# Two instructions of ScalarE moved behind a copy, and four half matmuls reordered, in the first attention of a fused attention-and-feed-forward kernel

## The chip, the cores and the metric

The kernel runs on one core of one Trainium2 chip. A core has five engines that run side by side, each in its own program order: TensorE (PE in the profile; its weight loads are PEld), VectorE (DVE), ScalarE (ACT), GpSimd (POOL) and SyncE (SP, which here only issues DMAs). They wait for one another through semaphores. The metric is the device time of one execution in microseconds (us).

## The reference

The input x has 2048 rows of 448. It is layer-normalised, and the result xn goes into two branches whose sum is added to x:

```python
xn = _layernorm(x)                                  # (x - mean) / sqrt(var + 1e-5)
# branch A: 16 heads of 28, causal attention over the last 256 positions
q, k, v = split(xn @ wqkv)
p = softmax(where(mask, q @ k.T * 28 ** -0.5, -1e9))
a = (p @ v) @ wo
# branch B
b = (gelu(xn @ w_gate) * (xn @ w_up)) @ w_down      # hidden width 1792
out = x + a + b
```

All arrays are bf16.

## The kernel before

The 2048 rows are 16 tiles of 128, handled in four blocks of 512 rows. For each block there is an attention stage (`attention`, 11 or 12 steps) and a gated feed-forward stage (`gated`); the other matmuls (q, k and v projections, up-projections, the previous block's down-projection) are fed into the attention steps so that PE has work while ACT computes exponentials. The order of instructions on every engine is the order in which the Python program emits them; there is no scheduler. Each engine runs its own in that order and waits at the first one whose input or buffer is not ready.

The width of 448 is three full chunks of 128 and one of 64. A projection is therefore three dense matmuls (`mm3`, L228) and one half matmul over 64 rows (`mm_half`, L233). Two half matmuls on different halves of the array can run at the same time, so halves are collected and issued in pairs ("excursions"): a generator yields HOLD after its dense part, and the next attention step first runs what is held. PE's results go to PSUM banks: tags "m" (two), "d" and "o" (one each), handed out in turn as m, m, d by `bank` during block 0. A bank is free again when the copy that empties it has run, on ACT or on DVE.

Block 0's attention has twelve steps, three for each group g of four heads. The one that the change touches is the beginning:

- Step 0 computes scores of group 0 (L600), the Exp on ACT (L604), zeroes masked entries on POOL (`masked`, L518), and feeds the dense q and k projections of group 1.
- Step 1 begins with the second excursion: the halves of q and k of group 1, and those of v for tiles 2 and 3, whose dense parts wait in banks "o" and "d"; then the copies out of PSUM: v of tile 3 on DVE (L253), q on ACT (L280), k on DVE (L281). Group 2's q projection takes bank "d", which v of tile 3 has held. After its scores, Exp and the dense projections of group 2, step 1 runs `ahead2`: statistics of tiles 6 and 7 on DVE (`stat`, L195 and L196), their reciprocal standard deviation on ACT (`rstd`: a Ln, L200, and an Exp, L201), the normalisation of tile 5 on DVE (`norm`, L209, a wide piece of 448 columns and a narrow one of 64) and its DMA transpose (L215, issued by SP).
- Step 2 begins with the third excursion, the halves of q and k of group 2 and their copies; then scores, Exp, and `ahead3` (norm and transpose of tiles 6 and 7, the copy of v of tile 2, and the loads of the remaining weights). Group 3's k projection takes bank "d", which group 2's q has held until its copy.
- At the end of steps 3 and 4 DVE runs `fill_pads`: nine small copies into unused columns of the q and k weights (L318 with 16 elements and L320 with 48, from `wraw` to `wqp` and `wkp`), and then three into `w3p` and a memset (L330). In steps 3 to 5 PE also computes up-projections (`ue`) of hidden chunks f = 2, 3, 8 and 9, which DVE casts into `hT` (L409), and the first `pv` (probabilities times v, L560), which DVE copies to `oc` (L570). From step 5 on follow the projections of block 1, v of tiles 4 and 5 first; v of tile 5 takes bank "d", which f = 8 has held.

The lines that only code can say, the bank order and the extra work of block 0:

```python
ring = [("m", "m", "d"), 0]
aux = [ahead, ahead2, ahead3, lambda: fill_pads(False), lambda: fill_pads(True), ...]
feeds = [Feed((gen_qk(0, (1, 2, 3), [(t, pvs[t]) for t in (2, 3)]), ...),
              (gen_up(0, (2, 8)), ...), (gen_proj(1), ...), (gen_up(0, (4,)), ...))]
```

Of the kernel before, what the change touches and what calls it, by code (L numbers as in the profile page):

```python
# [75 lines left out]
def kernel(  # L76
# [172 lines left out]
    def v_half(t, pv):  # L249
        mm_half(pv, xnT[:, 3, t * P:(t + 1) * P], wv[:, 3, :], t % 2, False, True)  # L250

    def v_copy(t, pv, copy):
        copy(out=v_sb[:, t, :, 0:Dh], in_=pv.rearrange("p (h d) -> p h d", d=Dh))  # L253
# [19 lines left out]
    def qk_halves(qb, g, pq, pk):  # L273
        w3 = w3p[:, 4 * g:4 * g + 4, :].rearrange("p h d -> p (h d)")
        for hi, ps in enumerate((pq, pk)):
            mm_half(ps, w3, xnT[:, 3, qb * QB:(qb + 1) * QB], hi, False, True)
# [7 lines left out]
    def gen_qk(qb, gs, others=()):  # L284

        for g in gs:
            pq = bank("pq")[:, :]
            proj(pq, wqp, qb, g)
            if qb and g == 3:
                yield 650  # L290
                ts = slice(qb * QB, (qb + 1) * QB)
                nc.tensor.matmul(pq, lhsT=w3p[:, 12:16, :].rearrange("p h d -> p (h d)"), rhs=xnT[:, 3, ts], start=False, stop=True,
                                 skip_group_check=True)
                nc.scalar.copy(out=qT[:, 3, ts], in_=pq)
                done.add((qb, 3))
                yield -220
                return
            yield 650
            pk = bank("pk")[:, :]
            proj(pk, wkp, qb, g)  # L300
            yield 650, HOLD
            qk_halves(qb, g, pq, pk)
            for t, pv in others:
                v_half(t, pv)
            if others:
                v_copy(*others[1], nc.vector.tensor_copy)
            qk_copies(qb, g, pq, pk)
            others = ()
            yield -360
# [211 lines left out]
    def attention(qb, feeds, aux, plan):  # L521
        oN = blk.tile([P, 4, QB], bf16, name="oN")
        oNs[qb] = oN
        parts, copied, inverses, later, fresh, behind = {}, [], [], [], [], []

        def scale_o(g, oc, inv):
            nc.gpsimd.tensor_tensor(out=oN[:, g, :], in0=oc[:, :], in1=inv, op=ALU.mult)  # L527

        def sums():

            g, oc = copied.pop(0)
            l1 = work.tile([P, 16, 32], f32, name="l1", tag="wc", bufs=1)
            ls = l_all[:, 4 * qb + g, :]
            nc.vector.transpose(out=l1[:, :, :].rearrange("p a b -> p (a b)"), in_=oc[:, :])  # L534
            nc.vector.tensor_copy(out=ls, in_=l1[:, :, Dh])
            ri = work.tile([P, 16], f32, name="ri")
            nc.vector.reciprocal(out=ri[:, :], in_=ls)
            inverses.append((g, oc, ri, l1))

        def inverse():  # L540

            g, oc, ri, l1 = inverses.pop(0)
            rb = l1 if qb else work.tile([P, 16, 32], f32, name="rb", tag="wb", bufs=1)
            nc.vector.transpose(out=rb[:, :, :], in_=ri[:, :].unsqueeze(2).to_broadcast([P, 16, 32]))  # L544
            later.append((g, oc, rb[:, :, :].rearrange("p a b -> p (a b)")))

        def add_halves(oc, ov):
            nc.scalar.copy(out=oc[:, :], in_=ov[0][:, :])  # L548
            nc.vector.tensor_tensor(out=oc[:, :], in0=oc[:, :], in1=ov[1][:, :], op=ALU.add)  # L549

        def pv(g):

            tags = ("o",) if not qb else ("m", "m" if g < 3 else down_tag[0])
            ov = [psum.tile([P, QB], f32, name="ov", tag=tag, bufs=2 if tag == "m" else 1) for tag in tags]
            todo = parts.pop(g)
            for n, (half, kt, q0, nq, col, p_sb) in enumerate(todo):
                k0 = 64 * half if half else 0
                r = slice(k0, k0 + (P if half is None else 64))
                for j in range(4):
                    nc.tensor.matmul(ov[half or 0][32 * j:32 * j + 32, q0:q0 + nq], lhsT=v_sb[r, kt, 4 * g + j, :],  # L560
                                     rhs=p_sb[r, j, col:col + nq], start=n == (half or 0), stop=n + len(tags) >= len(todo),
                                     tile_position=(k0, 32 * j), skip_group_check=True)
            oc = work.tile([P, QB], f32, name="oc", tag="wb" if qb and g % 2 else "wa", bufs=1)
            if qb:
                if g == 2:
                    behind.append((oc, ov))
                else:
                    add_halves(oc, ov)
            else:
                nc.vector.tensor_copy(out=oc[:, :], in_=ov[0][:, :])  # L570
            copied.append((g, oc))

        if qb:
            feeds[0].run()
        steps = list(steps_of(qb))
        pvs = {4: 0, 6: 1, 9: 2} if qb else {4: 0, 7: 1, 10: 2}
        for i, (scores, ncol, edges) in enumerate(steps):
            while (qb, scores[-1][0]) not in done:
                feeds[0].run()
            for fd in feeds:  # L580
                if fd.held:
                    fd.run()
            if i in pvs:
                pv(pvs[i])
            while fresh:
                apply_masks(*fresh.pop(0))
            if not qb and i - 1 in pvs:
                sums()
                inverse()
            if qb and i - 1 in pvs:  # L590
                sums()
            if qb and i - 2 in pvs:
                inverse()
            ss = phase[0].pool.tile([P, 4, QB], f32, name="sc", tag="s")
            p_sb = work.tile([P, 4, QB], bf16, name="p_sb", bufs=5)
            for g, half, kt, q0, nq, col in scores:
                k0, nk = (64 * half, 64) if half is not None else (0, P)
                for j in range(4):
                    r = slice(32 * j, 32 * j + Dh)
                    nc.tensor.matmul(ss[k0:k0 + nk, j, col:col + nq], lhsT=kT[r, g, kt * P + k0:kt * P + k0 + nk],  # L600
                                     rhs=qT[r, g, qb * QB + q0:qb * QB + q0 + nq], start=True, stop=True,
                                     tile_position=(32 * j, k0), skip_group_check=True)
                parts.setdefault(g, []).append((half, kt, q0, nq, col, p_sb))
            nc.scalar.activation(out=p_sb[:, :, 0:ncol], in_=ss[:, :, 0:ncol], func=ACT.Exp, scale=SCALE)  # L604
            while behind:
                add_halves(*behind.pop(0))
            if qb:
                fresh.append((p_sb, edges))
            else:
                for m in edges:  # L610
                    masked(p_sb, *m)
            while later:
                scale_o(*later.pop(0))
            left = len(steps) - i
            if left == 1:
                drain(feeds)
            elif not qb:
                share(feeds + [Feed()], 1e12, 0)
            else:
                to = plan.get(i, 0)  # L620
                whole = sum(f.left for f in feeds) + STEP * left + PV * sum(j > i for j in pvs)
                ahead = STEP + PV * (i + 1 in pvs) + (360 if to > 1000 else 0)
                late = 400 if i == 0 else 0
                want = (whole - late) / (left + 0.2) + late - ahead - to
                if i in pvs:
                    had = feeds[0].left
                    share(feeds[:1], min(1100, want), 0)
                    want -= had - feeds[0].left
                share(feeds, want, to)
            if aux:  # L630
                aux.pop(0)()

        def rest():
            while fresh:
                apply_masks(*fresh.pop(0))
            pv(3)

        def after(f):
            if inverses:
                inverse()  # L640
                scale_o(*later.pop(0))
            elif copied:
                sums()

        return rest, after
# [44 lines left out]
    pq, pk = (phase[0].pool.tile([P, 2, QB], f32, name="s0", tag="s")[:, 0, :] for _ in range(2))  # L690
# [23 lines left out]
    def ahead2():  # L714
        stat(6)
        stat(7)
        rstd(6, 2)
        norm(5)
        dma_transp(5)

# [211 lines left out]
```

## Time and profile before

| | |
|---|---|
| median of 3 runs | 223.24 us (223.16 to 223.36) |
| the profiled execution | 223.5 us |
| its span on the core | 221.7 us |
| PE busy | 214.3 us (97%) |
| DVE busy | 156.2 us (70%) |
| ACT busy | 132.9 us (60%) |
| POOL busy | 45.0 us (20%) |
| granted TensorE clock | 1.0 |

The span is the time from the first to the last instruction that the hardware profiler saw; the profiled execution's own time is 1.8 us longer. A line of a timeline has the start in us from the span's start, the duration in us, the engine, the source line, the operation, the tile written and those read, the shapes (partitions x elements), and how many instructions were merged; in brackets stands the idle time of the engine just before, and what ended it. In the chain of work that ended last, a line has start, length, engine, tile and source line. In the list of waits it has the waiting engine and instruction, what it waited for, us in total, how often, and the longest. The ends of matmuls are modelled.

### The profile page before, as it was taken

Reading aid. Unit: us, or ns where it says so; the run is one execution under the profiler, and the core shown is the slowest. Engines: PE = TensorE matmul, PEld = TensorE weight load, DVE = VectorE, ACT = ScalarE, POOL = GpSimd, SP = SyncE. Lnnn points to the kernel's source line nnn. Section 1 sums busy time; section 2 is a strip of 40 time slices with the busy share of each in tenths; the row PEclk is TensorE's granted clock in tenths of the full one; section 3 lists DMA queues with packets and bytes.
Section 4 is the critical chain, followed back from the end, with each engine's and each line's share of the span. In section 5 each row is a group of like instructions: output and inputs, shape, how many; then the busy total and the mean of one; then the engine's idle time right before and its main releaser. Section 6 shows DMA issues by size and latency. Waiting matters only on the chain.

```text
span 221.7 us, 5352 instructions
## 1 busy us (share of the span) xinstructions
PE 214.3 (97%) x2240; PEld 94.9 (43%) x2240; DVE 156.2 (70%) x370; ACT 132.9 (60%) x129; POOL 45.0 (20%) x65
## 2 busy tenths in 40 slices
PE   6999999999999999999999999999999999999992
PEld 2433333344444444444444445444344435444571
DVE  5889996799666983679566896495444899479320
ACT  4497788644878875432878886233567778464000
POOL 5773687320000220022000031022000022022000
PEclk9999999999999999999999999999999999999999
DMA  6997699104200001102500000200000000000011
GB/s 193 304 296 94 174 326 305 22 1 74 44 3 21 24 24 29 18 3 44 70 1 23 24 1 26 57 5 0 0 4 21 24 3 24 21 0 4 22 43 25
DMA packets 18044, 13.28 MB, mean 60 GB/s; under 512 B 8704, under 2 KB 16992, under 8 KB 18016
## 3 DMA queue, kind: packets, MB, share of 16 engines
q1 hardware_dynamic: 17072, 12.62, 22.6%
q8 instruction: 18, 0.29, 0.6%
q10 hardware_dynamic: 944, 0.29, 0.5%
q14 instruction: 10, 0.08, 0.1%
HBM read 9.15 MB, written 2.18 MB: 51 GB/s over the span
## 4 chain that ended last, share of the span: by engine, by line
PE 95%; DVE 2%; ACT 1%; POOL 0%; issue 0%; DVEq 0%
PE po L375 20%; PE gt L228 17%; PE u L228 12%; PE sc L600 6%; PE po L370 6%; PE gt L233 5%; PE ue L228 5%; PE ov L560 5%; PE pq L228 4%; PE pv L228 4%; PE pk L228 3%; PE wps L190 2%; PE pq L233 2%; PE ue L233 1%; PE pv L233 1%; PE s L228 1%
## 5 line engine op out<-in xcount | busy, mean ns | idle before, releaser
L604 ACT ACTIVATE p_sb<-sc 128x2048 bf16<-128x2048 f32 (+2 forms) x42 | 73.8, 1758 | 12.6 <-PE sc L600 7.3
L375 PE MATMUL po<-wd,hT 128*128 128x448 bf16 (+1 forms) x238 | 50.0, 342 | 0.0
L452 ACT ACTIVATE ge<-gt 128x1024 bf16<-128x1024 f32 x28 | 28.7, 1025 | 33.6 <-PE u L233 20.9
L527 POOL TENSOR_TENSOR oN<-oc,l 128x512 bf16<-128x512 f32 x12 | 16.0, 1332 | 138.6 <-DVE l L544 88.2
L228 PE MATMUL gt<-xnT,wg 128*128 128x512 bf16 x168 | 40.3, 380 | 0.0
L456 DVE TENSOR_TENSOR hT<-ge,u 128x512 bf16<-128x512 bf16 x40 | 25.6, 682 | 9.7 <-ACT ge L452 9.6
L375 PEld LDWEIGHTS <-hT 128*128 128x128 bf16 x238 | 21.4, 98 | 18.6 <-issue 2.6
L228 PE MATMUL u<-xnT,wu 128*128 128x512 bf16 x120 | 29.2, 379 | 0.0
L508 DVE TENSOR_TENSOR p_sb<-p_sb,masks 128x256 bf16<-128x256 bf16 (+1 forms) x90 | 27.2, 357 | 0.4 <-ACT p_sb L604 0.4
L228 PEld LDWEIGHTS <-wg 128*128 128x128 bf16 x168 | 15.1, 98 | 21.4 <-issue 5.2
L228 PEld LDWEIGHTS <-wu 128*128 128x128 bf16 x168 | 16.0, 98 | 19.2 <-issue 1.0
L549 DVE TENSOR_TENSOR oc<-oc,ov 128x512 f32<-128x512 f32 x12 | 8.3, 688 | 18.3 <-ACT oc L548 18.3
L600 PE MATMUL sc<-qT,kT 28*64 28x320 bf16 (+7 forms) x640 | 16.9, 263 | 0.1
L380 DVE TENSOR_TENSOR res<-po,x_sb 128x448 bf16<-128x448 f32 (+1 forms) x17 | 10.0, 586 | 8.7 <-PE po L375 8.6
L370 PE MATMUL po<-wo,oN 128*128 128x448 bf16 (+1 forms) x68 | 15.9, 342 | 0.0
L518 POOL TENSOR_SCALAR_AFFINE_SELECT p_sb<-p_sb 128x512 bf16<-128x512 bf16 (+1 forms) x20 | 14.3, 736 | 7.8 <-ACT p_sb L604 7.6
L409 DVE CAST hT<-ue 128x512 bf16<-128x512 f32 x16 | 10.2, 680 | 6.3 <-PE ue L233 6.2
L548 ACT COPY oc<-ov 128x512 f32<-128x512 f32 x12 | 7.0, 584 | 11.9 <-PE ov L560 11.9
L233 PE MATMUL gt<-xnT,wgu 64*128 64x512 bf16 x48 | 13.2, 379 | 0.0
L228 PE MATMUL pq<-xnT,wqp 128*128 128x512 bf16 x45 | 12.2, 380 | 0.3 <-DVE v_sb L253 0.3
L534 DVE STREAM_TRANSPOSE l<-oc 128x512 f32<-128x512 f32 x16 | 11.3, 704 | 1.4 <-POOL oN L527 1.2
L228 PE MATMUL ue<-xnT,wu 128*128 128x512 bf16 x48 | 12.0, 380 | 0.0
(87 smaller groups left out, 236.0 us busy)
## 6 DMA issues: line engine op xcount, KB each, us to landing
out_dram<-res SPq DMA_DIRECT2D x15, 112.0 KB
x_sb<-in_A_x_dram SPq DMA_DIRECT2D x3, 448.0 KB
wu<-in_B_w_up_dram SPq DMA_DIRECT2D x1, 1344.0 KB
wg<-in_B_w_gate_dram SPq DMA_DIRECT2D x1, 1344.0 KB
wd<-in_B_w_down_dram SPq DMA_DIRECT2D x3, 448.0 KB
wraw<-in_A_wqkv_dram SPq DMA_DIRECT2D x2, 252.0 KB
wo<-in_A_wo_dram SPq DMA_DIRECT2D x4, 98.0 KB
wv<-in_A_wqkv_dram SPq DMA_DIRECT2D x1, 336.0 KB
```

Source lines behind the costliest of these rows:

```text
L228: nc.tensor.matmul(ps, lhsT=lhs(c), rhs=rhs(c), start=start and c == 0, stop=stop and c == 2, skip_group_check=True)
L233: nc.tensor.matmul(ps, lhsT=lhs[p0:p0 + 64], rhs=rhs[p0:p0 + 64], start=start, stop=stop, tile_position=(p0, 0), skip_group_check=True)
L370: nc.tensor.matmul(po[:, 0:w], lhsT=oN[:, g, cs], rhs=wo[:, g, lo:up], start=(g == 0), stop=False, skip_group_check=True)
L375: nc.tensor.matmul(po[:, 0:w], lhsT=hT[:, f, cs], rhs=wd[:, f, lo:up], start=False, stop=(f == NF - 1), skip_group_check=True)
L452: nc.scalar.activation(out=ge[:, :, :], in_=pr["gt"][:, :, :], func=ACT.Gelu_apprx_tanh)
L456: nc.vector.tensor_tensor(out=hT[:, f + i, :], in0=ge[:, i, :], in1=u[:, :], op=ALU.mult)
L508: nc.vector.tensor_tensor(out=reg, in0=reg, in1=m, op=ALU.mult)
L518: nc.gpsimd.affine_select(out=reg, in_=reg, pattern=mid + [[1 if diag else -1, min(w, P)]], compare_op=ALU.is_ge, fill=0.0, base=0 if diag ...
L527: nc.gpsimd.tensor_tensor(out=oN[:, g, :], in0=oc[:, :], in1=inv, op=ALU.mult)
L534: nc.vector.transpose(out=l1[:, :, :].rearrange("p a b -> p (a b)"), in_=oc[:, :])
L600: nc.tensor.matmul(ss[k0:k0 + nk, j, col:col + nq], lhsT=kT[r, g, kt * P + k0:kt * P + k0 + nk], rhs=qT[r, g, qb * QB + q0:qb * QB + q0 + ...
L604: nc.scalar.activation(out=p_sb[:, :, 0:ncol], in_=ss[:, :, 0:ncol], func=ACT.Exp, scale=SCALE)
```

## The change

Two things in block 0's attention. In `gen_qk`, the halves of v for tiles 2 and 3 are issued ahead of the halves of q and k of group 1 (the order of the copies stays: v of tile 3, q, k). In `attention`, the Ln and Exp of `rstd(6, 2)` leave `ahead2`, where they stood ahead of group 2's q copy on ACT, and are emitted in step 2 after that copy and after the step's scores, just before the step's Exp.

```diff
             yield 650, HOLD
-            qk_halves(qb, g, pq, pk)
             for t, pv in others:
                 v_half(t, pv)
+            qk_halves(qb, g, pq, pk)
             if others:
                 v_copy(*others[1], nc.vector.tensor_copy)
             qk_copies(qb, g, pq, pk)
...
                 parts.setdefault(g, []).append((half, kt, q0, nq, col, p_sb))
+            if not qb and i == 2:
+                rstd(6, 2)
             nc.scalar.activation(out=p_sb[:, :, 0:ncol], in_=ss[:, :, 0:ncol], func=ACT.Exp, scale=SCALE)
...
     def ahead2():
         stat(6)
         stat(7)
-        rstd(6, 2)
         norm(5)
         dma_transp(5)
```

## The prediction

> **What bounds the kernel.** I read the page first (busy shares), then the waits by engine (here PE's), then the chain that ended last, and then the timelines of DVE, ACT, POOL and PE between 12 and 30 us, where the change lies.
>
> ```profile
> PE pk L228 <- ACT qT L280: 0.4, 1, 0.4
> PE pq L228 <- DVE v_sb L253: 0.3, 1, 0.3
> ```
>
> PE is busy for 97% of the span, and after the start it has only two named waits. Both lie in the first attention, at 15.43 and 18.54, and each part of the change aims at one. The chain shows more: between them it runs through DVE.
>
> ```profile
> 14.75 0.62 DVE v_sb L253
> 15.38 0.60 DVE kT L281
> ...
> 18.02 0.48 ACT qT L280
> 18.54 0.81 PE pk L228 x3
> ```
>
> So two engines have to be followed, not one. DVE has next to no gap from 14.75 until 24.30, and POOL's selects run beside it. DVE's timeline:
>
> ```profile
> 17.37 0.72 DVE L209 TENSOR_SCALAR xn<-x_sb,mv_all,rstd_all 128x448 bf16<-128x448 bf16 x1
> ...
> 21.77 0.15 DVE L318 COPY wqp<-wraw 128x16 bf16<-128x16 bf16 x1
> ...
> 22.02 0.67 DVE L409 CAST hT<-ue 128x512 bf16<-128x512 f32 x1
> ...
> 23.81 0.15 DVE L318 COPY w3p<-w3k 64x16 bf16<-64x16 bf16 x1
> ...
> 24.36 0.69 DVE L409 CAST hT<-ue 128x512 bf16<-128x512 f32 x1
> ```
>
> and POOL's:
>
> ```profile
> 12.89 0.24 POOL L161 TENSOR_SCALAR_AFFINE_SELECT masks<-masks 64x64 bf16<-64x64 bf16 x1
> 13.18 0.32 POOL L161 TENSOR_SCALAR_AFFINE_SELECT masks<-masks 64x64 bf16<-64x64 bf16 x1
> ...
> 17.32 0.64 POOL L518 TENSOR_SCALAR_AFFINE_SELECT p_sb<-p_sb 128x512 bf16<-128x512 bf16 x1
> ...
> 19.48 0.72 POOL L518 TENSOR_SCALAR_AFFINE_SELECT p_sb<-p_sb 128x512 bf16<-128x512 bf16 x1 [1.52 <-ACT p_sb L604]
> 22.14 1.10 POOL L518 TENSOR_SCALAR_AFFINE_SELECT p_sb<-p_sb 128x1024 bf16<-128x1024 bf16 x1 [1.93 <-ACT p_sb L604]
> ...
> 24.18 0.64 POOL L518 TENSOR_SCALAR_AFFINE_SELECT p_sb<-p_sb 128x512 bf16<-128x512 bf16 x1 [0.35 <-ACT p_sb L604]
> ```
>
> Three things are to be seen. First, DVE's SBUF-to-SBUF work and a POOL instruction hold each other up. The wide norm piece of tile 5 (17.37) takes 0.72 against a median of 0.38, and ends 0.13 after the select that started at 17.32. At 47.28 the same form takes 1.34 beside a POOL multiply and again ends 0.13 after it. Copies take part: POOL's select at 13.18 overlaps a weight copy (L653, 13.13) and takes 0.32 instead of 0.24. Second, whoever waits is next: the select of 19.48 waited for tile 7's wide piece, then went ahead of its narrow one, which ended 0.03 after it. Third, the pad copies of `fill_pads` (nine from 21.29 to 22.09, three more from 23.81 to 24.23) lie in holes between selects; POOL starts at 22.14, 0.05 after the ninth.
>
> **Part 1: v's halves first.** The same four matmuls run (0.39 and 0.35 us, in pairs), so PE's work is unchanged and no DMA moves. v's pair starts at 14.13 instead of 14.36 and ends 0.23 earlier. q's and k's pair starts at 14.33 (the pitch of a pair is 0.23 for 512 columns, so 0.20 for 448) and ends 14.72 instead of 14.52. DVE's v copy then starts at 14.53 instead of 14.75 and ends 15.15; PE's q projection of group 2, which needs that bank, starts at 15.20 instead of 15.43. ACT's q copy of group 1 slips from 14.67 to 14.75. What hides that: the next Exp waits for its scores until 15.21 anyhow, and starts at 15.24 (+0.02); POOL's selects move by the same. Without that cover the slip would cost 0.08.
>
> **Part 2: Ln and Exp behind the q copy.** They take 0.30 and 0.20; Ln starts at 17.49, because it waits for tile 7's statistics, and the q copy at 17.92. Freed from them the copy waits for its q half: 15.20 + 1.39 (the distance 15.43 to 16.82) + 0.39 + 0.04 = 17.01, and it ends at 17.60. Ln follows 0.47 after the copy's start (the distance from the copy at 36.93 to the Ln at 37.39), so at 17.49, and Exp at 17.81: rstd of tiles 6 and 7 is ready at 18.02, as before, and DVE wants it at 18.54. What now queues behind Ln is step 2's Exp; PE's scores of step 3 and POOL's select wait for it. It starts at 17.92 instead of 18.39 and ends at 18.95. PE's k projection starts at 17.79 instead of 18.54; step 3's scores wait for that Exp (18.95 + 0.05) and start at 19.00 instead of 19.61. Step 3's Exp starts at 19.45 instead of 20.19 and ends at 21.33. **POOL's first select of step 3 so moves from 22.14 to 21.40, 0.74 earlier.**
>
> **What DVE gains.** Its 0.23 reaches the norm of tile 5, whose wide piece now starts at 17.14, under the first of two selects (16.75 to 17.39, the second to 17.99). Bounds: it gets its turn between them and the narrow piece ends behind the second at 18.02 (-0.28), or it is held through both and the narrow piece ends at 18.32 (+0.02). I take the first, by the row at 19.48, where the one that waits is next. Tile 7's wide piece falls under step 2's select (19.02 to 19.66) instead of its narrow one, and the norm ends at 19.99 instead of 20.24. The v copy, the k copy and the pads follow: pads from 21.04 to 21.84, 0.25 earlier. SP's transposes of tiles 5 to 7 are issued by as much earlier, and PE wants tile 6 only at 26.39; the moved Ln and Exp issue no DMA.
>
> **The collision.** POOL moves by 0.74 and the pads by 0.25, so the select of 21.40 now starts inside the pads. Their 16-element copies start at 21.04, 21.28 and 21.52; the third comes 0.12 too late. No row shows a copy this small beside a running select. Bounds: it is not held (0), or held until the select ends (21.40 + 1.10 = 22.50, done 22.53 instead of 21.67). I take held: the narrow norm piece, as cheap, was held at 19.63, and the weight copy delayed POOL. The two 48-element copies after it start at 22.44 and 22.53, around the start of the second select (22.46); whether they too are held is the next unknown. I take not: L318 reads and writes four runs of four, in like rows on both sides as the weight copies do, while L320 reads three groups of four and writes twelve runs, a form that no row shows in contention.
>
> [...] No run here shows L320 beside a select.
>
> **The sum.** The first cast of `ue` starts at 22.61 instead of 22.02 and ends 23.28; PE's fourth up-projection needs its bank and starts at 23.33 instead of 23.19. The second cast and the copy of `oc` end at 24.48. Step 4's Exp runs 22.05 to 23.51 and its selects 23.57 to 24.80, so the 16-element copy of `w3p` (24.41, in a hole before) is held by the second and ends at 24.82; the memset ends 0.34 later, at 25.16. The cast of f=8 starts at 25.11 instead of 24.36 and frees its bank for the v projection of tile 5, which starts 0.05 after the cast ends: 25.85 instead of 25.11. That is **+0.75 us**. Behind it PE has no wait to give back, so it stays to the end: span 221.7 to 222.4, the profiled execution's 223.5 to 224.25. That execution stands 0.26 above the median of the runs, so the median goes from 223.24 to **224.0**.
>
> **Rivals.**
> - *The pads slip through* (other side): the third 16-element copy starts before the select or is not held. Place: 21.52 against 21.40; a shift of 0.1 decides. Then the pads end at 21.84, the memset at 24.05, the cast of f=8 runs 24.00 to 24.69 and the v projection starts at 24.75: -0.36, so 222.9. For it: no row shows so small a copy held. Against it: the narrow norm piece. Chance 0.20.
> - *Two holds*: also a 48-element copy, or a second 16-element one because tile 5's norm gained nothing. The first cast starts 23.04 to 23.20, the `w3p` copies then miss the selects, and the v projection starts at 26.02 to 26.19: +0.9 to +1.1, so 224.15 to 224.35. Chance 0.17.
> - *One hold, and `w3p` misses the second select* (needs a slip of 0.26 past 24.67): 25.59, +0.5, so 223.7. Chance 0.08.
> - *Only PE and ACT count*: the gain at step 3 (-0.61) lasts, 222.6. DVE's unbroken row of work speaks against it. Chance 0.03.
> - *Gain and hold cancel* (a copy held for a short rest of a select): 223.1 to 223.4. Chance 0.07.
>
> **How the numbers follow.** The forecast has 0.45, with 223.7 to 224.3 as its own range. A measurement of this kernel tells about 0.2% (0.45 us) from no change, so 222.79 and 223.69 are the bounds. Slower: 0.45 + 0.17 + half of the 0.08 = 0.66. Faster: 0.07 of the first rival and 0.02 of PE-and-ACT = 0.09. Same: the rest, 0.25. The range takes in both signs: 222.8 to 224.4.
>
> **What would show it.** Right: PE's two named waits are gone; q copy at about 17.0; POOL's 1024-element select near 21.4; a pad copy L318 of about 1 us; PE's `pv` of tile 5 near 25.85 with a new wait on DVE's cast. Wrong: all pad copies at 0.15 to 0.17, or the nine of them done before POOL starts.

## The result and the profile after

| | before | after |
|---|---|---|
| median | 223.36 us (223.16 to 223.52, 7 runs) | 224.20 us (223.87 to 224.46, 7 runs) |
| profiled execution | 223.5 us | 224.32 us |
| span of it | 221.7 us | 222.6 us |

The changed kernel takes 1.0036 times as long (95% interval 1.0024 to 1.0048): 0.84 us slower. The forecast was 0.75 us slower, 224.0.

What PE waits for in the first attention of the changed kernel:

```profile
PE ue L228 <- DVE hT L409: 0.6, 1, 0.6
PE pv L228 <- DVE hT L409: 0.6, 1, 0.6
```

Both waits that the change aimed at are gone. Two others have come, each longer than either of the old ones, and both are for DVE's casts of the up-projection. The timeline of the changed kernel shows where DVE lost the time:

```profile
17.05 0.58 ACT L280 CAST qT<-pq 128x512 bf16<-128x512 f32 x1 [0.34 <-PE pk L233]
...
17.18 0.36 DVE L209 TENSOR_SCALAR xn<-x_sb,mv_all,rstd_all 128x448 bf16<-128x448 bf16 x1
...
21.43 1.10 POOL L518 TENSOR_SCALAR_AFFINE_SELECT p_sb<-p_sb 128x1024 bf16<-128x1024 bf16 x1 [1.75 <-ACT p_sb L606]
21.47 0.16 DVE L320 COPY wkp<-wraw 128x48 bf16<-128x48 bf16 x1
21.55 1.00 DVE L318 COPY wqp<-wraw 128x16 bf16<-128x16 bf16 x1
...
22.64 1.27 DVE L409 CAST hT<-ue 128x512 bf16<-128x512 f32 x2
...
24.19 0.64 POOL L518 TENSOR_SCALAR_AFFINE_SELECT p_sb<-p_sb 128x512 bf16<-128x512 bf16 x1
24.43 0.42 DVE L318 COPY w3p<-w3k 64x16 bf16<-64x16 bf16 x1
...
25.22 0.69 DVE L409 CAST hT<-ue 128x512 bf16<-128x512 f32 x1
25.96 0.54 PE L228 MATMUL pv<-wv,xnT 128*128 128x448 bf16 x2 [0.58 <-DVE hT L409]
```

The last line is the v projection of tile 5. In the kernel before it started at 25.11:

```profile
25.11 0.35 PE L228 MATMUL pv<-wv,xnT 128*128 128x448 bf16 x1
```

A copy of 16 elements takes 1.00 us at 21.55 and 0.42 us at 24.43, against 0.15 before. Each started after the start of one of POOL's selects (21.43 and 24.19) and ended 0.02 to 0.03 us after its end. The 48-element copy at 21.47 started under the same select and took its usual 0.16. Note how this looks in a profile: the held copy counts as *busy*, no idle time is shown in front of anything on DVE, and the lists of waits name only the engine that waits for DVE. The timeline shows it only as a duration that is too long for the form, and the chain of work that ended last shows what it costs:

```profile
21.55 0.09 DVE wkp L320
21.63 0.92 DVE wqp L318
...
24.51 0.34 DVE w3p L318
```

0.92 and 0.34 us of the path belong to these two copies; the 16-element copies ahead of them have 0.08 each in the same chain.

### The profile page after: what moved, and what is told of

It reads as the page before. It is cut to its first block, busy times and chain, and to the rows that moved or that the text cites. A ratio compares the mean times of both kernels' runs of the same rounds, so it can differ in the third digit from the quotient of the medians.

```text
span 222.6 us, 5327 instructions
## 1 busy us (share of the span) xinstructions
PE 212.3 (95%) x2215; PEld 94.9 (43%) x2240; DVE 157.4 (71%) x370; ACT 132.9 (60%) x129; POOL 44.8 (20%) x65
## 4 chain that ended last, share of the span: by engine, by line
PE 90%; DVE 5%; issue 1%; ACT 0%; POOL 0%; DVEq 0%
PE po L375 20%; PE gt L228 17%; PE u L228 12%; PE po L370 6%; PE sc L600 6%; PE gt L233 5%; PE ov L560 4%; PE pq L228 4%; PE pv L228 4%; PE ue L228 3%; PE pk L228 3%; PE wps L190 2%; PE pq L233 1%; PE pv L233 1%; DVE xn L209 1%
## 5 line engine op out<-in xcount | busy, mean ns | idle before, releaser
L228 PE MATMUL gt<-xnT,wg 128*128 128x512 bf16 x161 | 38.9, 380 | 1.0 <-issue 0.9
L228 PE MATMUL pq<-xnT,wqp 128*128 128x512 bf16 x36 | 11.7, 380 | 0.5
```

Source lines behind the costliest of these rows:

```text
L228: nc.tensor.matmul(ps, lhsT=lhs(c), rhs=rhs(c), start=start and c == 0, stop=stop and c == 2, skip_group_check=True)
```

## Experiments

The theory: a select on POOL holds a 16-element copy on DVE until it ends, so what counts is whether POOL's selects or DVE's pad copies come first. Rivals: PE or DVE is late for another reason, and the long copy is only a symptom; or one part of the change does the harm by itself, through the later halves or through Ln and Exp in front of step 2's Exp.

The runs' starts differ: the first Exp of the attention begins between 12.82 and 13.10 us. Places are therefore also compared as a distance, from that Exp's start to the start of the v projection of tile 5 (12.21 before, 13.04 after), each from one profiled execution and worked out from unrounded starts.

| kernel | median, us | its before | ratio (95%) | Exp to v of tile 5 |
|---|---|---|---|---|
| changed | 224.20 | 223.36 | 1.0036 (1.0024 to 1.0048) | 13.04 |
| part 1 alone | 223.14 | 223.16 | 0.9990 (0.9981 to 0.9999) | 12.00 |
| part 2 alone | 224.53 | 223.16 | 1.0049 (1.0036 to 1.0063) | 13.26 |
| changed, 16-element copies first | 223.01 | 223.16 | 0.9987 (0.9978 to 0.9996) | 11.93 |
| changed, 16-element copies last | 224.13 | 223.16 | 1.0037 (1.0023 to 1.0050) | 13.20 |
| before, 16-element copies first | 223.32 | 223.15 | 1.0002 (0.9994 to 1.0011) | – |
| changed, w3p's copy in step 3 | 223.73 | 223.15 | 1.0029 (1.0019 to 1.0040) | 12.71 |
| changed, without two steps' selects | 222.97 | 223.15 | 0.9990 (0.9981 to 0.9999) | 11.94 |
| 16-element copies first, w3p's others on ACT | 222.79 | 223.15 | 0.9983 (0.9974 to 0.9991) | 11.77 |

The intervals of the ratios are about 0.4 to 0.6 us wide, so kernels that lie closer together than that are told apart by the distance alone. The distance can be trusted for this: in every profiled execution the end of PE's last matmul, counted from the first Exp, has moved against the kernel before by as much as the distance has, to 0.02 us. What follows the last matmul took between 3.98 and 4.40 us in these executions; the times contain that spread, the distances don't.

### Each part alone

Part 1 alone is the first hunk of the diff, part 2 alone the other two.

> Part 1 alone: v's halves first; Ln and Exp of tiles 6 and 7 stay ahead of group 2's q copy. Theory of the collision: the q copy then starts at about 17.7 instead of 17.92, step 3's Exp moves by no more than DVE does (0.2), POOL's 1024-element select starts near 21.9 and the nine pad copies (21.05 to 21.85) stay ahead of it, each 0.15 to 0.17 us. The whole stretch moves by DVE's 0.2: 0.2 us faster than before, 223.1 to 223.2. Rival (the loss comes from q's and k's halves being later): slower than before, by some part of the 0.84.

> Part 2 alone: Ln and Exp behind the q copy; q's and k's halves stay ahead of v's. Theory of the collision: the q copy at about 17.24, step 2's Exp at 18.14, step 3's Exp ends at about 21.55 and POOL's 1024-element select starts near 21.62 instead of 22.14, while DVE has gained next to nothing (pads from 21.25). The third 16-element copy is held until about 22.7, and the w3p copy under step 4's second select: slower by 0.8 to 1.0 us, more than both parts together. Rival (part 2 takes PE's wait of 0.4 away and part 1 does the harm): faster by 0.1 to 0.4.

Part 1 alone: the distance falls by 0.21, and the time is 0.9990 of that before. POOL's select comes at 22.14 again, and the ninth pad copy (21.89 to 22.05) is out of the way before. Its timeline:

```profile
21.73 0.16 DVE L318 COPY wqp<-wraw 128x16 bf16<-128x16 bf16 x1
...
22.14 1.10 POOL L518 TENSOR_SCALAR_AFFINE_SELECT p_sb<-p_sb 128x1024 bf16<-128x1024 bf16 x1 [1.97 <-ACT p_sb L604]
```

The select was expected near 21.9; since this execution started 0.21 late, 22.14 stands for 21.93. Part 2 alone is dearer than both together by the distance, which grows by 1.05 (in time 1.37 us between the medians, more than was expected, with an interval that overlaps that of the changed kernel), and the held copies are there again:

```profile
21.94 0.97 DVE L318 COPY wqp<-wraw 128x16 bf16<-128x16 bf16 x1
...
24.79 0.42 DVE L318 COPY w3p<-w3k 64x16 bf16<-64x16 bf16 x1
```

So the harm is part 2's, the part that takes PE's larger wait (0.4 us) away. It brings POOL forward and DVE not at all; part 1 brings DVE forward by 0.2 and so gives a little of it back. That q's and k's halves come later costs nothing that can be seen.

### The order of the copies

In the changed kernel, `fill_pads` is split into a 16-element copy and a 48-element one, and the calls are put in another order:

```diff
+        def wide(dst, src):      # the 16-element copy, as L318
...
+        def narrow(dst, src, lo):    # the 48-element copy, as L320
...
         if not last:
             for c in range(3):
-                put(wqp[:, c, :, :], k, 4, 0)
-                put(wkp[:, c, :, :], k, 3, 4)
+                wide(wqp[:, c, :, :], ks[c])
+            wide(w3p[0:64, :, :], w3k[0:64, :])
+            for c in range(3):
+                narrow(wqp[:, c, :, :], ks[c], 0)
+                narrow(wkp[:, c, :, :], ks[c], 4)
             return
...
```

> The changed kernel, with the four 16-element pad copies (three of wqp, one of w3p) run first at the end of step 3, and the 48-element ones after them. Same copies, same DVE work. Theory (16-element copies are held by a running select, 48-element ones are not): the four are done at about 21.4, before the select of 21.43; the 48-element copies run beside the select at 0.16 each; the first cast starts near 21.9 and the v projection of tile 5 near 24.9: 0.2 us faster than before, 1.0 faster than the changed kernel. Rival A (every copy is held): the 48-element copies that start after 21.43 are held, about as slow as the changed kernel or slower. Rival B (the held copy is a symptom, PE is late for another reason): 224.2, unchanged.

> The changed kernel, with the three 16-element copies of wqp behind the six 48-element ones; the w3p copies stay at the end of step 4. Theory: all three start after the select of 21.43. The first is held to 22.55; the second slips in between the two selects; the third is held by the second select to about 23.1. The first cast starts near 23.1, and w3p's copies then miss step 4's selects: the v projection of tile 5 starts near 26.2, +1.1 us on before. If both remaining copies slip in between: +0.86 as in the changed kernel. Rival B (symptom): 224.2.

With the 16-element copies first, the loss is gone and a gain has taken its place: 13.04 falls to 11.93. In its timeline (the 16-element copies are L316 here, the 48-element ones L321) the four start before the select, the last ending 0.01 us after its start, and the 48-element copies run beside it as if it were not there:

```profile
20.96 0.30 DVE L316 COPY wqp<-wraw 128x16 bf16<-128x16 bf16 x3
21.18 0.15 DVE L316 COPY w3p<-w3k 64x16 bf16<-64x16 bf16 x1
...
21.32 1.10 POOL L522 TENSOR_SCALAR_AFFINE_SELECT p_sb<-p_sb 128x1024 bf16<-128x1024 bf16 x1 [1.75 <-ACT p_sb L610]
...
21.42 0.16 DVE L321 COPY wqp<-wraw 128x48 bf16<-128x48 bf16 x1
...
21.67 0.16 DVE L321 COPY wkp<-wraw 128x48 bf16<-128x48 bf16 x1
```

Both rivals of that run fall: not every copy is held, and the long copy was no symptom.

With the 16-element copies last, all three start after the start of the select:

```profile
21.55 0.98 DVE L316 COPY wqp<-wraw 128x16 bf16<-128x16 bf16 x1
...
22.45 0.64 POOL L522 TENSOR_SCALAR_AFFINE_SELECT p_sb<-p_sb 128x512 bf16<-128x512 bf16 x1
22.51 0.60 DVE L316 COPY wqp<-wraw 128x16 bf16<-128x16 bf16 x1
```

The first is held to 22.53 by the select of 21.40, the second (not shown, 22.44 to 22.60) slips in between the two selects, and the third is held by the second select to 23.11. The w3p copy then finds no select in its way (0.15 at 24.82). The distance grows by 0.99, where 1.1 was expected; the order of the holds is the expected one. The time, 224.13, can't be told from the changed kernel's, and an unchanged time is what the rival "symptom" forecast; it is the trace that speaks for the holds here.

The control puts the same order into the kernel before:

> The kernel before, with only the pad copies reordered as in the experiment with the 16-element copies first. Theory: nothing is held in the kernel before, so the order of the copies is worth nothing: within 0.1 us of before; PE's v projection of tile 5 as far behind the first Exp as before (12.2 us). Rival (the reorder is a gain by itself, whatever the selects do): faster by as much as the reorder gained in the changed kernel, 0.8 us or more.

The ratio is 1.0002, with an interval that spans no change and leaves out the rival's 0.8 us: without a collision the order is worth nothing that these runs can tell. The median is 0.17 above its before, a little more than the 0.1 expected. The expected distance can't be read, because in the profiled execution a load of weights landed late (DVE waited 0.97 us for it), and the distance there is 14.01.

### Each hold by itself

In the changed kernel, w3p's 16-element copy is moved from step 4 to the front of step 3's pad copies:

```diff
         if not last:
+            nc.vector.tensor_copy(out=w3p[0:64, 12:16, Dh:32],
+                                  in_=w3k[0:64, :].rearrange("p (j d) -> p j d", d=Dh)[:, :, 24:28])
             for c in range(3):
...
-        put(w3p[0:64, :, :], w3k[0:64, :], 4, 0)
+        put(w3p[0:64, :, :], w3k[0:64, :], 3, 0)
```

> The changed kernel, with only w3p's 16-element copy moved, from the end of step 4 to the front of step 3's pad copies. Theory: the third 16-element copy of wqp is still held (to about 22.55), but the second hold, 0.27 us under step 4's second select, is gone: the v projection of tile 5 starts near 25.6 instead of 25.96, 0.5 us slower than before, 0.3 faster than the changed kernel. If the extra copy in front pushes the second 16-element copy past the select's start too, two are held and the time is 0.8 to 1.1 slower than before. Rival (one hold alone makes the whole loss): as the changed kernel, 0.84 slower.

The copy in front delayed the others by 0.07, and the second 16-element one of wqp just got through (21.31, the select at 21.35); the third was held (21.55 to 22.48). The distance is 12.71, so 0.50 over before, and the second hold is worth the other 0.33. The 0.50 is what the first hold leaves over after the change's own gain, not its whole price: against the changed kernel without any hold (11.94, the next experiment) the first hold costs 0.77 and both 1.10.

The next experiment leaves POOL's selects of steps 3 and 4 out of the changed kernel:

```diff
-                for m in edges:
+                for m in edges if i not in (3, 4) else ():
                     masked(p_sb, *m)
```

> The changed kernel without POOL's selects of steps 3 and 4 of block 0: the causal mask of heads 4 to 7 is left out for keys 0 to 255 of the first 512 rows. Nothing else is changed, the pad copies stay where they are. Theory: no select is there to hold a copy; all twelve pad copies take 0.15 to 0.18 us, the v projection of tile 5 starts near 24.8, 0.3 us faster than before. Rival (the 16-element copy is late for a reason of its own, such as DVE's waits or its operands): the copy still takes about 1 us and the time stays at 0.8 slower.

With no select there, the very same copies in the same places take 0.15 to 0.17 us:

```profile
21.62 0.15 DVE L318 COPY wqp<-wraw 128x16 bf16<-128x16 bf16 x1
...
23.66 0.15 DVE L318 COPY w3p<-w3k 64x16 bf16<-64x16 bf16 x1
```

The distance is 11.94, the same as with the copies in a better order (11.93). POOL's select is the cause, shown from both sides: the loss goes when the copies are moved out of its way, and when the select is taken out of theirs. It also shows what the change is worth without a hold: PE's two old waits, 0.7 us in all, are gone, and the v projection of tile 5 comes 0.27 us earlier.

### A version that is faster than both

Against the version with the 16-element copies first (`narrow` gets the copying engine as an argument):

```diff
-        narrow(w3p[0:64, :, :], w3k[0:64, :], 0)
-        narrow(w3p[64:128, :, :], w3k[64:128, :], 4)
+        narrow(w3p[0:64, :, :], w3k[0:64, :], 0, nc.scalar.copy)
+        narrow(w3p[64:128, :, :], w3k[64:128, :], 4, nc.scalar.copy)
         nc.vector.memset(w3p[64:128, 12:16, :], 0.0)
```

> The version with the 16-element copies first, and besides w3p's two 48-element copies on ACT instead of DVE (in ACT's gap between step 4's and step 5's Exp). Theory: with the holds gone DVE's chain bounds the v projection of tile 5; 0.3 to 0.35 us less on it lets the cast of f=8 start when PE's halves are done, and the v projection starts near 24.5: 0.5 to 0.55 us faster than before, 0.25 faster than with the order alone. ACT's two copies of about 0.25 each delay step 5's Exp by up to 0.5, which nobody waits for before step 7. Rival (DVE is no longer the bound, or ACT's delay comes out at step 6): no faster than with the order alone.

It takes 222.79 us, 0.36 us below its before (ratio 0.9983), against 0.15 below with the order alone (0.9987; the two intervals overlap, so that it beats the order alone rests on the distance, 11.77 against 11.93). By the distance that is 0.44 faster than before, less than the 0.5 to 0.55 expected. The two copies on ACT take 0.47 together:

```profile
23.37 0.47 ACT L321 COPY w3p<-w3k 64x48 bf16<-64x48 bf16 x2
24.03 1.02 ACT L610 ACTIVATE p_sb<-sc 128x1024 bf16<-128x1024 f32 x1 [0.19 <-PE sc L604]
```

ACT has a gap of 0.19 left behind them, so step 5's Exp was not delayed. The v projection starts at 24.64, where 24.5 was expected: DVE, with its memset still in front of the cast, bounds it by a little even now. PE's halves are done at 23.70, the memset ends at 23.86, and the cast starts at 23.89.

## Why the prediction was right

The direction, the size and the place were right, and the likeliest case was the one that happened.

- **Part 1 and part 2.** The q copy starts at 17.05 (forecast 17.01), Ln's pair ends at 18.07 (18.02), and nothing waits for it; step 3's select starts at 21.43 (21.40). All these are 0.03 to 0.05 late, 0.03 of it because this execution's attention started 0.03 later.
- **What DVE gains.** Of the two bounds for tile 5's norm, the one chosen holds: the wide piece starts at 17.18 under the first select and takes 0.36, as it does at 4.93 where POOL is idle. It ends 0.13 after the first select's end (17.41), and the second select takes 0.67 instead of 0.63, so the wide piece got its turn between the two. The narrow piece is held by the second select (0.61 instead of 0.29) and ends at 18.07, 0.23 earlier than before. The rows of the kernel before had only shown this the other way round, with POOL waiting.
- **The collision.** This was the unknown, and "held" was right: 21.55 to 22.55, forecast 21.52 to 22.53. So was "not held" for the 48-element copies. No run of the kernel before shows it: the start of the first cast in the sum (22.61) rests there on the author's estimate. What the runs showed in its place: L320 takes 0.16 beside the select (at 21.47) and the cast starts at 22.64, while L318 takes up to 1.00. What sets the two apart is not shown, because no run changes one property of the copies alone. In these runs it is not the number of elements by itself: 16 are held, 48 are not, and the 64 of the norm's narrow piece are held again (0.61 instead of 0.29). With the 48-element copies taken as held, the forecast would have been the rival of two holds, +0.9 to +1.1 where the distance grew by 0.83. The times could hardly have told the two apart (224.15 to 224.35 there, 224.20 measured); the 48-element rows do.
- **The sum.** Forecast +0.75, measured +0.85 between the two profiled executions at the v projection of tile 5 (25.11 and 25.96; 0.83 by the distance), and +0.84 in the medians. The term that was too small is the last one: I let the cast of f=8 start 0.05 before the memset in front of it ends, much as the pad copies and the cast behind them do in the kernel before (each starts 0.07 to 0.08 before the end of the one in front), but it starts 0.03 after it (25.19 and 25.22), as with the 16-element copies first (23.97 and 24.00). The fourth up-projection behaves as written: 23.36, forecast 23.33.
- **It stays to the end.** PE's last matmul ends 0.84 later, counted from the first Exp, as it was 0.83 later at the v projection. Nothing between them gave anything back.
- **The rivals.** Three of the five turned up in an experiment, near their price by the distance: the pads slipping through, forecast -0.36 (measured -0.27 without selects and -0.28 with the other order, but only -0.18 and -0.15 in the medians); one hold with w3p missing the second, +0.5 (+0.50, median +0.58); two holds, +0.9 to +1.1 (+0.99, median +0.97). "Only PE and ACT count" never appeared: with part 2 in the kernel, DVE's chain set the start of the v projection in every profiled execution, while before and with part 1 alone the cast waited for PE's halves. A gain and a hold that cancel did not appear either.

## What to carry to other kernels

When a change makes one engine earlier, list what runs beside it on the other engines in the next ten microseconds and move each by its own shift: here POOL moved by 0.7 us and DVE by 0.2, and two streams that had passed each other with 0.05 us to spare collided. A wait that an engine gets rid of is worth only what the second-longest chain allows, and a short instruction that is held by another engine's instruction can cost as much as what is left of that one: here 1.00 us for a copy of 0.15, with 0.98 of the select left. Where such instructions can't be moved apart, their order within the group may be enough (a distance of 11.93 instead of 13.04), and part of the group on another engine may add a little (11.77).

## What was not expected of the hardware

That waiting DVE work gets through between two of POOL's selects that the profile shows without a gap (the second starts 0.04 to 0.05 before the first ends) was only inferred beforehand. It shows twice: the wide norm piece of 17.18 in the changed kernel (0.36, with the second select starting at 17.37), and the 16-element copy of 22.44 to 22.60 in the run with the copies last, which got through right behind the held one, while the next, 0.07 later, had to wait out the whole second select. In these traces a hold goes with which record starts first. The 16-element copies that got through at the start of a select started ahead of it, the closest at 22.44 against 22.45; the seven that were held started 0.06 to 0.24 us behind it, and all seven ended 0.02 to 0.03 us after its end. (Two that started in a select's last 0.06 us took their usual time: 0.15 at 23.81 in the kernel before, and 0.16 at 22.44 with the copies last.) So how long a held copy took went with what was left of the select: 0.93 to 1.00 us under the selects of 1.10, and 0.42 to 0.60 under those of 0.64.
